# Four weight matrices, each by one transfer onto 96 partitions, in a decode kernel (attention and MLP mixer, one core)

## The chip, the cores and the metric

The kernel runs on one core of one Trainium2 chip. The metric is the device time of one execution in microseconds (us). Before the change it is 215.7 us, the median of three runs (215.67 to 217.24).

## The reference

Four tokens (batch B = 4, one position, D = 576) go through a layer norm. The result `xn` feeds two branches, whose outputs are added to `x`.

```python
xn  = layernorm(x)
out = x + A(xn) + Bm(xn)
# A: sliding-window attention over a cache, 32 query heads, 16 KV heads, Dh = 128
q = xn @ wq                      # 576 x 4096
k, v = last 2048 positions of k_cache, v_cache   # of 8192
A = softmax(q k^T / sqrt(128)) v @ wo            # 4096 x 576
# Bm: mixer MLP
h  = gelu(layernorm(xn) @ w1)    # 576 x 576
hs = shift(h) @ w2               # one position only: every shifted part is zero
x1 = xn + hs
Bm = x1 + gelu(layernorm(x1) @ w3) @ w4          # 576 x 4608, 4608 x 576
```

With one position the shifted `h` is all zeros, so the product with `w2` has a zero operand; the kernel still loads `w1` and `w2` and multiplies. All data is bf16.

## The kernel before, in words

The kernel is written as a list of operations for each engine (`prog`), each with a sort key, a list of events to wait for and an event that it signals. `add` (L163) and `add_dma` (L167) fill the lists, the lists are sorted by key (L543), and each engine then runs its list in order. An operation that waits holds everything behind it on its engine. Keys, not the order in the file, set the order of the work. All transfers but that of `x` and half of the output are issued by SP, in one queue.

**Buffers.** `kring` (L69) and `vring` (L70) are rings with four slots each (NKS, NVS); a slot has UE = 8192 bf16 for each of 128 partitions and holds one KV head of K or V, 2 MB. `regB` (L72) holds transposed K (`ktbuf`, 16 slots). Before the heads arrive the same memory holds the weights: `wq`, `w1` and `w2` lie in the V ring (L79 to L90), `w3` in `regB` (L77, L78), later `wo` in the K ring (L81) and `w4` in the V ring (L242).

**A weight with 576 rows on 128 partitions.** 576 is four and a half times 128. Rows 0 to 511 go to 128 partitions, four consecutive rows each (the "main" part); the last 64 rows are split into halves of columns, so that (row, half) makes 128 short rows (the "rag" part, `rag_src`, L178). `wq` and `w3` come by three transfers each (rows r = 0 and 1, rows 2 and 3, the rag; L215 to L218 and L221 to L224), `w1` and `w2` by two (L219, L220). The stationary operand has to match: `ragsrc` (L103) holds the last 64 columns of the normed tokens twice, spread over even and odd columns, with zeros between. Two copies in `ln_ops` (L266, L267) write it behind each of the three norms, and `pe_xT` (L270) makes six small transposes, four of the main part and two of `ragsrc`.

**Order of the first part.** On SP: `wq`, `w1`, `w2`, `w3` (keys -20 to -8), K0 to K3 without a wait, then K4 and on, each waiting until its slot was transposed (L230 to L232). V0 goes in after K8 (V0_AFTER), V1 to V15 after K15; V0 to V2 wait for `hs1`, as the weights lie in those slots, and V4 and on wait for the head that used the slot before (L236). `wo` follows V3. On TensorE: transposes of the first and second norm's result, `q` in five pieces that each wait for their part of `wq` (`pe_q`, L286, L299), the transposes of q, `hT` (`w1`, L472) and `hs0`, `hs1` (`w2`, L481), the transposes of the third norm, `h2` in five pieces (`pe_h2`, L501), then `pe_zeroS` (L318), which opens the score sums in PSUM and waits for all that used those banks. Then the loop over K: for each head 64 transposes (`pe_T`, L327), which VectorE and ScalarE copy to `ktbuf` (`evac`, L337), and 16 score matmuls (`pe_SC`, L343) for the head before.

**After K.** One softmax for all heads (L374 to L410), then the loop over V (`pe_PV`, L412), `wo` (`pe_AO`, L443) and `w4` (L527), and the two halves of the output.

## Time and profile before

| | |
|---|---|
| median of three runs | 215.7 us |
| the profiled execution | 215.64 us |
| its span, first to last instruction | 214.4 us |
| instructions | 5735 |
| TensorE matmul busy | 143.2 us, 67% |
| weight load busy | 109.1 us, 51% |
| VectorE, ScalarE, GpSimd busy | 84.5, 59.1, 10.0 us |
| read from HBM | 88.49 MB |
| mean clock granted to TensorE | 0.785 |

How to read it. Times are microseconds unless marked ns. PE is TensorE's matmul, PEld its weight load, DVE VectorE, ACT ScalarE, POOL GpSimd, SP SyncE; SPq is the instructions by which SP issues transfers. L332 is line 332 of the kernel. "out<-in" are the tensors written and read, xN the number of instructions. A time and a duration at the start of a line are the start from the beginning of the span and the length; in brackets stands how long the engine sat idle before and what ended that. The chain of work that ended last is followed back from the last instruction, at each step to what released it. The DMA and GB/s rows give the span in 40 equal slices of 5.36 us. A stretch of the windows view gives, in order, the bounds, the length, busy time and count of each engine (PE, PEld, DVE, ACT, POOL), the granted clock, the share of the 16 DMA engines that was busy, and GB/s.

### The profile page before, as it was taken

Reading aid. Unit: us, or ns where it says so; the run is one execution under the profiler, and the core shown is the slowest. Engines: PE = TensorE matmul, PEld = TensorE weight load, DVE = VectorE, ACT = ScalarE, POOL = GpSimd, SP = SyncE. Lnnn points to the kernel's source line nnn. Section 1 sums busy time; section 2 is a strip of 40 time slices with the busy share of each in tenths; the row PEclk is TensorE's granted clock in tenths of the full one; section 3 lists DMA queues with packets and bytes.
Section 4 is the critical chain, followed back from the end, with each engine's and each line's share of the span. In section 5 each row is a group of like instructions: output and inputs, shape, how many; then the busy total and the mean of one; then the engine's idle time right before and its main releaser. Section 6 shows DMA issues by size and latency. Waiting matters only on the chain.

```text
span 214.4 us, 5735 instructions
## 1 busy us (share of the span) xinstructions
PE 143.2 (67%) x2646; PEld 109.1 (51%) x2648; DVE 84.5 (39%) x162; ACT 59.1 (28%) x71; POOL 10.0 (5%) x34
## 2 busy tenths in 40 slices
PE   0368375999999993999999719813343443973655
PEld 0115223777788883788877604813343443463523
DVE  5502603666666663466666479411111112100000
ACT  2000302566555553365666653000000000000000
POOL 8101000000010000000000000000000000000000
PEclk9999755999999999699999985555555555585589
DMA  6999999999999999999999999999999999999992
GB/s 245 434 395 439 440 410 437 428 408 431 428 431 422 431 428 434 422 434 423 431 425 431 428 407 411 424 427 431 419 434 431 431 419 434 428 434 421 424 412 113
DMA packets 7697, 88.63 MB, mean 413 GB/s; under 512 B 764, under 2 KB 1032, under 8 KB 2824
## 3 DMA queue, kind: packets, MB, share of 16 engines
q1 hardware_dynamic: 7672, 88.50, 97.8%
q8 instruction: 7, 0.11, 0.2%
q14 instruction: 2, 0.02, 0.0%
q10 hardware_dynamic: 16, 0.01, 0.0%
HBM read 88.49 MB, written 0.00 MB: 413 GB/s over the span
## 4 chain that ended last, share of the span: by engine, by line
DMA 53%; PE 36%; DVE 4%; SPq 4%; issue 2%; ACT 0%
DMA vring<-in_A_v_cache_dram 25%; PE ps L332 23%; DMA kring<-in_A_k_cache_dram 21%; PE ps L348 7%; DMA vring<-in_B_w_dram 7%; PE ps L416 5%; SPq L174 4%; DVE PTb L382 1%; DVE rmax L374 1%; DVE regB L340 1%; PE ps L441 1%; DVE PTs L390 1%; PE ps L405 0%; ACT P_sb L379 0%; DVE out_sb L539 0%
## 5 line engine op out<-in xcount | busy, mean ns | idle before, releaser
L340 DVE COPY regB<-ps 128x1024 bf16<-128x1024 bf16 x80 | 52.3, 687 | 34.7 <-PE ps L332 32.9
L332 PEld LDWEIGHTS ps<-perm_k,kring 128*128 128x128 bf16 x1024 | 58.7, 99 | 12.6 <-issue 8.7
L332 PE MATMUL ps<-perm_k,kring 128*128 128x128 bf16 x1024 | 62.1, 222 | 4.2 <-DMA kring<-in_A_k_cache_dram 4.2
L339 ACT ACTIVATE regB<-ps 128x1024 bf16<-128x1024 bf16 x48 | 47.7, 1023 | 41.4 <-PE ps L332 41.4
L416 PE MATMUL ps<-PTg,vring 128*128 128x8 bf16 x1024 | 29.2, 168 | 33.3 <-DMA vring<-in_A_v_cache_dram 31.4
L416 PEld LDWEIGHTS ps<-PTg,vring 128*128 128x128 bf16 x1024 | 28.1, 103 | 34.5 <-DMA vring<-in_A_v_cache_dram 24.3
L424 DVE TENSOR_TENSOR OTn<-ps,rinvB 128x8 bf16<-128x8 f32 x16 | 2.7, 167 | 57.3 <-PE ps L416 57.2
L540 ACT ACTIVATE out_sb<-ps 4x288 bf16<-4x288 f32 x1 | 0.4, 402 | 81.2 <-PE ps L441 81.2
L348 PE MATMUL ps<-regB,Qs 128*32 128x512 bf16 x272 | 18.7, 395 | 4.6 <-issue 3.5
L348 PEld LDWEIGHTS ps<-regB,Qs 128*32 128x32 bf16 x272 | 6.6, 97 | 10.8 <-issue 6.2
L393 DVE TENSOR_TENSOR PTg<-PTs,bmask 128x512 bf16<-128x512 bf16 x16 | 10.7, 682 | 0.0
L370 POOL COPY Qs<-Qpad 128x128 bf16<-128x128 bf16 x16 | 4.6, 296 | 93.5 <-PE ps L348 81.4
L441 PE MATMUL ps<-kring,ORT 128*4 128x288 bf16 x64 | 7.7, 431 | 0.7 <-DVE ORT L458 0.7
L441 PE MATMUL ps<-vring,h2T_sb 128*4 128x288 bf16 x72 | 5.3, 299 | 2.8 <-DMA vring<-in_B_w_dram 2.8
L511 PE MATMUL ps<-regB,x1nT 128*32 128x432 bf16 (+1 forms) x60 | 5.4, 522 | 2.1 <-DMA regB<-in_B_w_dram 1.6
L274 PE MATMUL ps<-ident_bf,xn_bf 4*128 4x4 bf16 x8 | 0.5, 169 | 8.8 <-DVE ragsrc L267 8.8
L296 PE MATMUL ps<-vring,xnT 128*32 128x512 bf16 x40 | 4.6, 629 | 1.8 <-DMA vring<-in_A_wq_dram 1.8
L441 PEld LDWEIGHTS ps<-kring,ORT 128*4 128x4 bf16 x64 | 3.8, 121 | 3.9 <-DVE ORT L458 0.9
L441 PEld LDWEIGHTS ps<-vring,h2T_sb 128*4 128x4 bf16 x72 | 3.0, 87 | 5.3 <-DMA vring<-in_B_w_dram 4.0
L383 PE MATMUL ps<-PTb,perm_p 128*128 128x512 bf16 x3 | 1.8, 608 | 4.9 <-DVE PTb L382 4.8
L274 PEld LDWEIGHTS ps<-ident_bf,xn_bf 4*128 4x128 bf16 x8 | 0.4, 112 | 8.8 <-POOL ones_f L210 6.3
L524 DVE STREAM_TRANSPOSE h2T_sb<-PTb 128x1152 bf16<-128x1152 bf16 x1 | 1.4, 1378 | 8.4 <-ACT PTb L521 8.4
(88 smaller groups left out, 61.7 us busy)
## 6 DMA issues: line engine op xcount, KB each, us to landing
kring<-in_A_k_cache_dram SPq DMA_DIRECT2D x16, 2048.0 KB, 16.1
vring<-in_A_v_cache_dram SPq DMA_DIRECT2D x16, 2048.0 KB, 17.6
regB<-in_B_w_dram SPq DMA_DIRECT2D x2, 2304.0 KB, 21.3
kring<-in_A_wo_dram SPq DMA_DIRECT2D x1, 4608.0 KB, 24.1
vring<-in_A_wq_dram SPq DMA_DIRECT2D x2, 2048.0 KB, 9.5
vring<-in_B_w_dram SPq DMA_DIRECT2D x2, 2016.0 KB, 15.7
vring<-in_B_w_dram SPq DMA_DIRECT2D x2, 576.0 KB, 13.8
vring<-in_B_w_dram SPq DMA_DIRECT2D x1, 864.0 KB, 14.7
```

Of the source, the lines that this page charges most:

```text
L174: e.dma_start(o_, i_).then_inc(S[skey], 16)
L296: ins = e.matmul(Qps[32 * j:32 * j + 32, k, :], lhsT=x_, rhs=w, start=(r == 0), stop=(r == 4), tile_position=(0, 32 * j))
L332: ins = e.transpose(tb[n % NTB][:, t, :], kring[:, g % NKS, 8 * k + t, :], perm_k[:])
L339: return "act", lambda e: e.activation(out=ktbuf[:, n % NKT], in_=src, func=ACTF.Copy)
L340: return "dve", lambda e: e.tensor_copy(out=ktbuf[:, n % NKT], in_=src)
L348: ins = e.matmul(Sps[32 * b:32 * b + 32, c4, :].rearrange("p (t i) -> p t i", t=16), lhsT=Qs[:, g % 4, b, :], rhs=kttile[:, t0:t0 + 16, b, :],
L370: P(lambda e, g=g: e.tensor_copy(out=Qs[:, g % 4], in_=Qpad[:, g]), waits=(["qT"] if g == 0 else []) + ([f"SC{g - 4}"] if g >= 3 else []), ...
L393: add("dve", lambda e, g=g: e.tensor_tensor(out=PTg[:, g % NPG], in0=PTs[:, :, 2 * g:2 * g + 2].unsqueeze(2).to_broadcast([128, NT, B, 2]) ...
L416: ins = e.matmul(OTps(g), lhsT=vring[:, g % NVS, t, :], rhs=PTg[:, g % NPG, t].rearrange("p b e -> p (b e)"), start=(t == 0), stop=(t == N ...
L424: add("dve", lambda e, g=g: e.tensor_tensor(out=OTn[:, 8 * g:8 * g + 8], in0=OTps(g), in1=rinvB[:, 8 * g:8 * g + 8], op=ALU.mult), waits=[ ...
L441: return e.matmul(ACC[h], lhsT=lhsT, rhs=rhs, start=start, stop=stop, tile_position=(0, 32 * h))
L511: ins = e.matmul(H2ps[k][32 * j:32 * j + 32, :], lhsT=x_, rhs=w, start=(r == 0), stop=(r == 4), tile_position=(0, 32 * j))
```

## The change

`wq`, `w1`, `w2` and `w3` each come by one transfer: 576 = 96 x 6, so 96 partitions (`KP`) get six consecutive rows each, and partitions 96 to 127 nothing. There is no rag part, and `ragsrc`, its memset and its copies go. Every product with these weights is a sum over six rows instead of four and a remainder. `wq` lies in slots 1 to 3 of the K ring, `w1` and `w2` in slot 0, `w3` in the V ring. So K0 waits for `hs1`, K1 to K3 wait for `q`, and V0 to V3 for `h2`. `q` and `h2` are one operation each, which waits for the whole weight. Slots 8 to 15 of `ktbuf`, which held `w3` before, are set to zero by GpSimd (`kt_zero`), and `pe_zeroS` waits for that: the first score matmuls read them.

```diff
-        regB_t = sb("regB", [128, max(NKT * 1024, W3E)], BF16)
+        regB_t = sb("regB", [128, NKT * 1024], BF16)
...
+        w3_sb = vring_t[0:KP, 0:6 * F].rearrange("p (r n) -> p r n", r=6)
+        wq_sb = kring_t[0:KP, UE:UE + 6 * Hq * Dh].rearrange("p (r n) -> p r n", r=6)
+        w1_sb = kring_t[0:KP, 0:6 * D].rearrange("p (r n) -> p r n", r=6)
+        w2_sb = kring_t[0:KP, 6 * D:12 * D].rearrange("p (r n) -> p r n", r=6)
...
-        xnT = sb("xnT", [128, 6, 32], BF16)
+        xnT = sb("xnT", [KP, 6, 32], BF16)
...
-        def rag_src(w_ap):
-            return w_ap[512:576, :].rearrange("r (h n) -> (r h) n", h=2)
+        def rows6(w_ap):
+            return w_ap.rearrange("(p r) n -> p r n", r=6)
...
-        P(lambda e: e.memset(ragsrc[:], 0.0), sig="rag_zero", key=-97)
...
+        P(lambda e: e.memset(ktbuf[:, 8:16, :], 0.0), sig="kt_zero", key=-88)
...
-        for r in (0, 2):
-            ev_wq += 2 * [add_dma([(wqmain[:, r:r + 2, :], wq_src[:, r:r + 2, :])], ("wq", r), (), -20 + r)]
-        ev_wq.append(add_dma([(wqrag, rag_src(A_wq))], ("wq", 4), (), -15))
...
+        ev_wq, ev_w1, ev_w2, ev_w3 = [add_dma([(d_, rows6(s_))], nm, (), -20 + k) for k, (nm, d_, s_) in enumerate(
+            (("wq", wq_sb, A_wq), ("w1", w1_sb, B_w1), ("w2", w2_sb, B_w2), ("w3", w3_sb, B_w3)))]
...
-                                [f"T{8 * (g - NKS) + 7}"] if g >= NKS else [], g))
+                                [f"T{8 * (g - NKS) + 7}"] if g >= NKS else ["hs1" if g == 0 else "q"], g))
...
-            w = [f"PV{g - NVS}"] if g >= NVS else (["hs1"] if g < WQ_SLOTS else [])
+            w = [f"PV{g - NVS}"] if g >= NVS else ["h2"]
...
-            add("dve", lambda e: (e.tensor_copy(out=ragsrc[:, idx, 0, 0:128:2], in_=dst[:, 512:D]),
-                                  e.tensor_copy(out=ragsrc[:, idx, 1, 1:128:2], in_=dst[:, 512:D]))[1],
-                waits=[f"{tag}_n", "rag_zero"], sig=tag, key=k0 + 0.05)
...
+        def pe_q(e):
+            ins = None
+            for k in range(2):
+                for r in range(6):
+                    for j in range(4):
+                        c0 = 1024 * j + 512 * k
+                        ins = e.matmul(Qps[32 * j:32 * j + 32, k, :], lhsT=xnT[:, r, :], rhs=wq_sb[:, r, c0:c0 + 512],
+                                       start=(r == 0), stop=(r == 5), tile_position=(0, 32 * j))
+            return ins
+        add("pe", pe_q, waits=[ev_wq, "xnT"], sig="q", key=-30)
...
-        add("pe", pe_zeroS, waits=["zeros_bf", "perm_k", "gelu2", "gelu_h", "qT", "x1nT", "x1"], sig="zeroS", key=-1)
+        add("pe", pe_zeroS, waits=["zeros_bf", "perm_k", "gelu2", "gelu_h", "qT", "x1nT", "x1", "kt_zero"], sig="zeroS", key=-1)
...
+        add("pe", pe_h2, waits=[ev_w3, "x1nT", "qT"], sig="h2", key=KW)
```

`pe_hT`, `pe_hs` and `pe_h2` change in the same way as `pe_q`: one loop over r = 0 to 5.

## The prediction

> **What bounds the kernel now.** I read the page first: the span, the DMA rate in 40 slices, the queue table.

> ```profile
> span 214.4 us, 5735 instructions
> GB/s 245 434 395 439 440 410 437 428 408 431 428 431 422 431 428 434 422 434 423 431 425 431 428 407 411 424 427 431 419 434 431 431 419 434 428 434 421 424 412 113
> q1 hardware_dynamic: 7672, 88.50, 97.8%
> ```

> Every slice but the first and the last moves 395 to 440 GB/s, and nearly all of the traffic is in one queue, SP's. 88.5 MB have to pass through it. The end therefore moves with two things only: a hole in that queue, or a change of the pace at which it drains. The chain of work that ended last shows who feeds whom:

> ```profile
> 8.87 27.18 DMA kring<-in_A_k_cache_dram
> 36.05 0.13 issue
> 36.18 1.83 PE ps L332 x16
> 38.02 0.98 PE ps L348 x16
> 38.99 3.71 PE ps L332 x64
> ...
> 43.99 3.71 PE ps L332 x64
> ```

> K0 was issued at 8.87 and landed at 36.05: 27 us, nearly all of it behind the weights. From then on TensorE takes one K head every 5.00 us (38.99 to 43.99). The pace in that stretch of the span (last column GB/s, before it the share of the 16 DMA engines):

> ```profile
> 36.00:66.00 30.00, 28.58 (x470) 23.95 (x471) 18.43 (x29) 16.41 (x17) 1.78 (x6) 0.97 1.01 427
> ```

> A head of K is 2048 KB (row below), 2.097 MB, so 4.91 us at 427 GB/s: DMA and TensorE run almost level, TensorE 0.09 us a head slower, and V0, put in after K8, gives TensorE the time back. SP's own list of issues (start, length of the run, how many) tells how far ahead the queue is filled:

> ```profile
> 0.81 1.34 SPq L174 DMA_DIRECT2D vring<-in_A_wq_dram  x3
> ...
> 8.87 53.45 SPq L174 DMA_DIRECT2D kring<-in_A_k_cache_dram  x9
> 62.36 0.60 SPq L174 DMA_DIRECT2D vring<-in_A_v_cache_dram  x1
> ...
> 116.69 0.39 SPq L174 DMA_DIRECT2D kring<-in_A_wo_dram  x1
> 134.27 48.11 SPq L174 DMA_DIRECT2D vring<-in_A_v_cache_dram  x12
> ```

> K0 to K3 were issued together, V0 after K8, wo once K14 was transposed, V4 once V0 was used up. The first slice's 245 GB/s are 1.31 MB, 3.0 us at 434, so the first byte moved at about 2.3, 1.5 us after the first issue.

> **The change part by part.** *The four weights on 96 rows.* Their sizes, with those of K and wo (KB each, then the time from issue to landing):

> ```profile
> kring<-in_A_k_cache_dram SPq DMA_DIRECT2D x16, 2048.0 KB, 16.1
> regB<-in_B_w_dram SPq DMA_DIRECT2D x2, 2304.0 KB, 21.3
> kring<-in_A_wo_dram SPq DMA_DIRECT2D x1, 4608.0 KB, 24.1
> vring<-in_A_wq_dram SPq DMA_DIRECT2D x2, 2048.0 KB, 9.5
> vring<-in_B_w_dram SPq DMA_DIRECT2D x2, 576.0 KB, 13.8
> regB<-in_B_w_dram SPq DMA_DIRECT2D x1, 576.0 KB, 25.8
> vring<-in_A_wq_dram SPq DMA_DIRECT2D x1, 512.0 KB, 12.5
> vring<-in_B_w_dram SPq DMA_DIRECT2D x2, 72.0 KB, 13.5
> ```

> The weights (wq 4096 + 512, w1 and w2 1152 + 144, w3 4608 + 576) are 11088 KB, 11.35 MB; at 427 GB/s 26.6 us. All of these transfers lie on 128 partitions, as K and V do. The new ones put the same bytes on 96, a third more on each. The trace has no large transfer on fewer than 128 partitions, so I bound the cost. If the 16 engines set the pace and share the 96 rows (six each), the stream still takes 26.6 us: cost 0. If it is the partition that sets the pace, nothing in this trace shows one filled faster than 427 / 128 = 3.34 GB/s; 96 of them take 320 GB/s, the stream 35.5 us: cost +8.9. If, beyond that, two engines keep meeting at the same partitions' input and halve each other, it is up to twice, 53.2 us: cost +26.6. I take +8.9, because the one rate that the trace shows, on every large transfer, belongs to 128 evenly filled partitions, and a gap there is not refilled: the queue is full all the way to the end.

> [...]

> *Fewer transfers.* Ten issues become four, and the 72 KB ones with short rows go. That SP issues sooner is worth nothing, since its first transfer still starts at 0.81 and the queue is never empty. The short rows cost pace: slices three and six (395 and 410 GB/s beside 434 to 440) lose 0.52 and 0.33 us of their 5.36. Not all of it is theirs; between 0 and 0.85 I take 0.4 gained.

> *The matmul work.* Six rows instead of four and a remainder: wq 40 matmuls to 48, w1 and w2 10 to 12 each, w3 60 to 72, and each starts only when its whole weight is in, no longer in pieces:

> ```profile
> 9.36 1.90 PE L296 MATMUL ps<-vring,xnT 128*32 128x512 bf16 x16
> 13.04 2.75 PE L296 MATMUL ps<-vring,xnT 128*32 128x512 bf16 x24 [1.78 <-DMA vring<-in_A_wq_dram]
> 17.62 1.12 PE L476 MATMUL ps<-vring,xn2T 128*4 128x288 bf16 x4
> 19.97 1.05 PE L484 MATMUL ps<-vring,hs_inT 128*4 128x288 bf16 x4
> 21.47 0.29 PE L485 MATMUL ps<-vring,hs_inT 128*4 128x288 bf16 x1
> 28.63 2.11 PE L511 MATMUL ps<-regB,x1nT 128*32 128x432 bf16 x24 [1.12 <-DMA regB<-in_B_w_dram]
> 31.19 1.15 PE L511 MATMUL ps<-regB,x1nT 128*32 128x432 bf16 x12 [0.45 <-DMA regB<-in_B_w_dram]
> 32.39 1.26 ACT L521 ACTIVATE PTb<-ps 128x432 bf16<-128x432 f32 x3 [5.07 <-PE ps L511]
> 34.10 1.49 PE L321 MATMUL ps<-zeros_bf 128*128 128x512 bf16 x3 [1.76 <-ACT PTb L521]
> ```

> The last piece of w3 is used from 31.19; it comes at 31.2 - 0.4 + 8.9 = 39.7. Then 72 matmuls at 2.11 / 24 = 0.088 us, 6.3 us, to 46.0; the gelu (1.26, with its hand-over 1.4) to 47.4; the zeroing of the scores, which ended 1.9 us after the gelu (33.65 to 35.59), to 49.3. K0 has been there since 39.7 + 4.9 = 44.6. So the first transpose of K is at 49.3 instead of 36.18, 13.1 us late, of which only 8.5 are the stream's. What hides the other 4.6: K4 is issued when K0 is transposed, 5.6 us after the first transpose (36.18 to 38.99 plus three quarters of 3.71), at 54.9, while K3 lands at 39.7 + 4 x 4.9 = 59.3. The queue has 4.4 us in hand, less the 1.5 from issue to first byte, and loses 0.09 a head until V0. After that TensorE has this slack as well:

> ```profile
> PE ps L332 <- DMA kring<-in_A_k_cache_dram: 4.2, 2, 3.6
> ```

> At V0 it stood still for 3.6 us; that wait shrinks to nothing and the K phase ends some 13.1 - 3.6 = 9.5 late. V4, issued at 134.27, goes out at 143.8; wo, issued at 116.69 and 24.1 us under way, lands near 140.8 + 8.5 = 149.3. So V4 is in time and the end moves with DMA alone. Without this cover each late microsecond would be one at the end.

> *The waits.* K0 now waits for hs1, K1 to K3 for q, V0 for h2. Behind K0 on SP stand K1 to K3 and everything later, and TensorE's first transpose waits for K0. hs1 ended at 21.76 (21.47 + 0.29). wq's last piece, issued at about 1.7 and 12.5 under way, was in at 14.2; with the stream at 4/3 wq is in at 14.2 + 3.7 = 17.9. Sixteen matmuls took 1.90, so 48 take at most 5.7, and q ends at 23.6 instead of 15.8 (13.04 + 2.75). The four matmuls more of w1 and w2 before hs1 add 2 x 0.235 (17.62 to 19.97 is ten) and 2 x 0.18 (19.97 to 21.76): 0.8. hs1 comes at 21.76 + 7.8 + 0.8 = 30.4, long before w3 leaves the queue at about 39. Cost nothing; w3 behind it in the queue is the cover. V0, issued at 62.36, and h2, done at 46.0, do not meet.

> *GpSimd and VectorE.* One memset and six copies go, a memset of 128 x 8192 comes.

> ```profile
> 2.19 2.31 DVE L404 COPY bmask<-bmask 128x4 f32<-128x4 f32 x1
> 2.65 1.82 POOL L193 MEMSET Qpad<- 128x2080 bf16 x1
> 8.28 0.42 DVE L264 TENSOR_SCALAR xn_bf<-xn_bf,mv,rstd 4x576 bf16<-4x576 bf16 x1
> ```

> At 1.82 us for 2080 columns the new one takes 7.2, from about 5.4 to 12.6. The tiny copy that lasted 2.31 us and ended with the Qpad memset suggests that VectorE's SBUF copies stand still meanwhile; then the second norm's last step slips from 8.28 to 12.6, and the transposes before q to about 13.4. wq lands at 14.2 at the earliest: cost nothing, with 0.8 us in hand, or 4.5 with the slow stream. Each norm is also 0.3 to 0.5 us shorter without its copies, which the wait for wq or w3 hides.

> Sum, against the profiled execution's own 215.64 us (span 214.4 and 1.2 around it; the median of the runs shown is 215.7): 215.6 + 8.9 - 0.4 = **224.1 us**.

> **The rivals.**

> *No loss: the engines share 96 rows as well as 128.* For it: the DMA share is 1.01 in the quoted stretch, so all 16 engines are busy, and six rows each is an even split. Against it: no row shows them at this pace into fewer partitions. It decides if wq lands before about 15 us. q then ends at 14.2 + 5.7 = 19.9, hs1 is at 21.76 + 4.1 + 0.8 = 26.7, K0's first byte at about 28.2 and w3 through at 31.2 - 0.4 = 30.8, so the queue has no hole; the transposes start 13.1 - 8.5 = 4.6 us late and are covered as above. Time 215.6 - 0.4 = 215.2: not slower.

> *The new gate becomes the bound.* The same fast stream, but q late, because the memset holds up both norms instead of one: the first norm then ends after 12.6, the second needs its 2 us once more, q starts at about 16 and hs1 is at 28.5. From about 29 on K0 comes after w3 has left, and each microsecond is a hole. Against it: the first norm's end precedes the memset in the list of before. Time 215.2 + 0 to 4, about 217.

> *Uneven meeting.* Rows are 48 and 54 KB long, so an engine stays on one row for longer than now (16 and 18 KB); engines that meet stay together, the last of 16 sets the landing, and the fast ones run ahead into K and then starve. [...] Against: any arbitration that spreads. Up to twice: 215.2 + 26.6 = 242; halfway from the forecast, 233.

> **How the numbers follow.** Forecast (even slowing, 220 to 229) 0.46; no loss 0.17; the gate 0.06; uneven meeting 0.27; anything else, such as more than twofold slowing, 0.04. No loss and half of the gate lie within 1% (what a measurement of this kernel can tell from no change): 0.17. Over 1% faster would need more than the 0.85 us of short rows: 0.02. Slower: 0.81. The range goes from the no-loss case with the whole 0.85 us, 214.8, to 240, which leaves out the top of the uneven case; the forecast's own is 220 to 229.

> **What would show it.** Right: fewer GB/s, some 320, in the slices up to about 38 us and 427 to 434 after; q starting near 18, the last w3 matmuls from about 39.7, the first K transpose near 49; TensorE's wait at V0 gone. Wrong: wq in at 14 (no loss), K0's issue after w3 has landed (gate), or w3 in after 45 (uneven). If holes appear in K's slices after 50, the cover that I counted on was too thin.

## The result and the profile after

The changed kernel takes 242.96 us, the median of five runs (241.75 to 244.83), beside 215.72 us before (215.67 to 217.24). The ratio is 1.1235, with a 95% interval of 1.1164 to 1.1306: slower by 12%. The profiled execution took 241.91 us with a span of 240.6. The forecast was 224.1 us, the range 214.8 to 240.0; the result lies outside it. In the ratios here and below, executions more than 1.5% above the fastest of the same kernel are left out.

The page of the changed kernel, span, DMA share and rate in 40 slices (now of 6.0 us each):

```profile
span 240.6 us, 5773 instructions
DMA  9796979879999999999999999999999999999992
GB/s 238 155 261 135 354 156 269 175 150 376 428 417 425 429 425 433 425 422 430 433 426 433 425 425 428 408 413 437 419 430 430 428 425 433 422 433 428 427 411 115
```

From the tenth slice on this is the picture of before. The first nine slices, in which the weights come, swing between 135 and 354 (a long packet seems to be counted whole where it starts: between 25 and 30 us the windows view gives a DMA share of 1.57) and are on average far below it. The windows view evens this out when a stretch takes in the whole weight stage. Here it is of the kernel before, up to the last weight, and then of the changed kernel; the last columns are the share of the 16 DMA engines and GB/s:

```profile
2.00:31.00 29.00, 14.88 (x134) 6.62 (x134) 10.56 (x34) 3.87 (x8) 4.82 (x14) 0.88 0.99 414
```

```profile
2.00:56.40 54.40, 13.42 (x98) 7.47 (x98) 16.32 (x28) 3.88 (x8) 10.97 (x14) 0.84 0.97 213
60.00:90.00 30.00, 27.64 (x431) 21.44 (x424) 16.59 (x25) 14.74 (x17) 1.48 (x5) 0.89 1.01 426
90.00:120.00 30.00, 28.04 (x472) 23.11 (x470) 18.99 (x30) 17.41 (x18) 1.76 (x6) 1.00 1.01 428
```

The reader is to see two columns together. In the weight stage the engines are busy for 0.97 of the time, as good as always, yet they move 213 GB/s instead of 414. They are not idle or starved: together they work at half their pace. With K the same engines move 426 to 428. The issues, KB each and time to landing:

```profile
vring<-in_B_w_dram SPq DMA_DIRECT2D x1, 5184.0 KB, 53.5
kring<-in_A_wq_dram SPq DMA_DIRECT2D x1, 4608.0 KB, 25.2
kring<-in_B_w_dram SPq DMA_DIRECT2D x2, 648.0 KB, 28.4
```

wq takes 25.2 us from issue to landing; in the kernel before, its last piece was in at about 14.2. The timelines of TensorE and of SP's issues carry it on:

```profile
26.05 5.31 PE L267 MATMUL ps<-kring,xnT 96*32 96x512 bf16 x48 [9.51 <-DMA kring<-in_A_wq_dram]
56.41 5.95 PE L477 MATMUL ps<-vring,x1nT 96*32 96x432 bf16 x72 [15.45 <-DMA vring<-in_B_w_dram]
63.73 1.89 PE L291 MATMUL ps<-zeros_bf 128*128 128x512 bf16 x4 [1.36 <-ACT PTb L486]
65.41 1.57 PE L302 MATMUL ps<-perm_k,kring 128*128 128x128 bf16 x16
37.55 53.72 SPq L162 DMA_DIRECT2D kring<-in_A_k_cache_dram  x9
158.97 49.64 SPq L162 DMA_DIRECT2D vring<-in_A_v_cache_dram  x12
```

w3 is in at 56.41 instead of 31.19, 25.2 us late. The first transpose of K is at 65.41 instead of 36.18, 29.2 late; by V4's issue (158.97 instead of 134.27) the lateness is 24.7, and most of the difference went into TensorE's waits for K, which shrank from 4.2 us (3.6 of them at V0) to 0.9; the end is 26.3 late (241.91 - 215.64). Of these 26.3 us, 25.2 are there when w3 lands. What the V phase adds, 1.6 us, is less than the spread of the five runs (3.1 us), and I do not explain it.

### The profile page after: what moved, and what is told of

The parts are those of the page before. It is cut to its first block, busy times and chain, and to the rows that moved or that the text cites. A ratio compares the mean times of both kernels' runs of the same rounds, so it can differ in the third digit from the quotient of the medians.

```text
span 240.6 us, 5773 instructions
## 1 busy us (share of the span) xinstructions
PE 146.8 (61%) x2672; PEld 111.8 (46%) x2672; DVE 90.2 (38%) x156; ACT 59.4 (25%) x71; POOL 16.1 (7%) x34
## 3 DMA queue, kind: packets, MB, share of 16 engines
q1 hardware_dynamic: 6680, 88.49, 97.8%
## 4 chain that ended last, share of the span: by engine, by line
DMA 46%; PE 39%; another core or an unknown queue 6%; DVE 5%; issue 2%; ACT 1%
DMA vring<-in_A_v_cache_dram 23%; PE ps L302 20%; DMA kring<-in_A_wq_dram 10%; DMA kring<-in_A_k_cache_dram 7%; DMA vring<-in_B_w_dram 6%; PE ps L318 6%; PE ps L386 4%; PE ps L477 2%; PE ps L267 2%; PE ps L446 1%; DVE PTb L352 1%; DVE rmax L344 1%; PE ps L291 1%; PE ps L454 1%
## 5 line engine op out<-in xcount | busy, mean ns | idle before, releaser
L302 PEld LDWEIGHTS ps<-perm_k,kring 128*128 128x128 bf16 x1024 | 58.0, 98 | 9.0 <-issue 7.3
L386 PEld LDWEIGHTS ps<-PTg,vring 128*128 128x128 bf16 x1024 | 28.3, 103 | 36.4 <-DMA vring<-in_A_v_cache_dram 24.8
L318 PE MATMUL ps<-regB,Qs 128*32 128x512 bf16 x272 | 17.8, 381 | 4.2 <-issue 2.9
L477 PE MATMUL ps<-vring,x1nT 96*32 96x432 bf16 (+1 forms) x72 | 6.0, 526 | 15.4 <-DMA vring<-in_B_w_dram 15.4
L477 PEld LDWEIGHTS ps<-vring,x1nT 96*32 96x32 bf16 x72 | 2.6, 146 | 18.3 <-DMA vring<-in_B_w_dram 15.5
L267 PE MATMUL ps<-kring,xnT 96*32 96x512 bf16 x48 | 5.3, 630 | 9.5 <-DMA kring<-in_A_wq_dram 9.5
L252 PE MATMUL ps<-ident_bf,xn_bf 4*96 4x4 bf16 x12 | 1.9, 268 | 14.7 <-DVE xn_bf L244 14.7
L489 DVE STREAM_TRANSPOSE h2T_sb<-PTb 128x1152 bf16<-128x1152 bf16 x1 | 1.4, 1378 | 22.5 <-ACT PTb L486 22.5
L252 PEld LDWEIGHTS ps<-ident_bf,xn_bf 4*96 4x96 bf16 x12 | 1.7, 221 | 14.7 <-POOL regB L198 12.6
L411 PE MATMUL ps<-vring,h2T_sb 128*4 128x288 bf16 x72 | 6.4, 343 | 1.6 <-DMA vring<-in_B_w_dram 1.6
L267 PEld LDWEIGHTS ps<-kring,xnT 96*32 96x32 bf16 x48 | 1.7, 141 | 12.3 <-DMA kring<-in_A_wq_dram 9.6
L198 POOL MEMSET regB<- 128x8192 bf16 x1 | 6.9, 6921 | 0.0
## 6 DMA issues: line engine op xcount, KB each, us to landing
kring<-in_A_k_cache_dram SPq DMA_DIRECT2D x16, 2048.0 KB, 15.1
vring<-in_A_v_cache_dram SPq DMA_DIRECT2D x16, 2048.0 KB, 17.6
vring<-in_B_w_dram SPq DMA_DIRECT2D x1, 5184.0 KB, 53.5
kring<-in_A_wq_dram SPq DMA_DIRECT2D x1, 4608.0 KB, 25.2
kring<-in_A_wo_dram SPq DMA_DIRECT2D x1, 4608.0 KB, 25.6
vring<-in_B_w_dram SPq DMA_DIRECT2D x2, 2016.0 KB, 16.1
vring<-in_B_w_dram SPq DMA_DIRECT2D x1, 864.0 KB, 14.7
```

The costliest lines, as they stand in the source:

```text
L198: P(lambda e: e.memset(ktbuf[:, 8:16, :], 0.0), sig="kt_zero", key=-88)
L252: ins = e.transpose(XTps[idx][:, r, :], v[:, r, :], ident_bf[0:B, 0:B])
L267: ins = e.matmul(Qps[32 * j:32 * j + 32, k, :], lhsT=xnT[:, r, :], rhs=wq_sb[:, r, c0:c0 + 512], start=(r == 0), stop=(r == 5), tile_posit ...
L302: ins = e.transpose(tb[n % NTB][:, t, :], kring[:, g % NKS, 8 * k + t, :], perm_k[:])
L318: ins = e.matmul(Sps[32 * b:32 * b + 32, c4, :].rearrange("p (t i) -> p t i", t=16), lhsT=Qs[:, g % 4, b, :], rhs=kttile[:, t0:t0 + 16, b, :],
L386: ins = e.matmul(OTps(g), lhsT=vring[:, g % NVS, t, :], rhs=PTg[:, g % NPG, t].rearrange("p b e -> p (b e)"), start=(t == 0), stop=(t == N ...
```

## The experiments

Two theories were set against each other after the result. Theory P: it is the partitions; with 96 of them the engines meet at the same inputs of the on-chip memory. (An input here is a path by which data of the DMA engines enters a group of partitions; that there are such shared paths is part of the theory, and the last run tests it.) The rivals: L, it is the long packets (48 and 54 KB instead of 16 and 18); S, it is where the engines read in HBM; and later E, an engine is simply slow in any load that does not have 128 partitions.

**Two rows per transfer** (`e1_two_rows`). The diffs of this part show the changed pieces of lines.

```diff
-add_dma([(d_, rows6(s_))], nm, (), -20 + k)
+add_dma([(d_[:, r:r + 2, :], rows6(s_)[:, r:r + 2, :]) for r in (0, 2, 4)], nm, (), -20 + k)
```

> The changed kernel with each of the four weights in three transfers of two rows per partition, still on 96 partitions. A packet is then 16 or 18 KB, as in the kernel before, instead of 48 or 54 KB. Theory P (the partitions: with 96 of them the 16 engines meet two by two at the same input): nothing changes, w3 in at about 56 us and 243 us in all. Rival L (the long rows: a packet of 48 KB moves at half the rate of one of 16 KB): the stream is back at 427 GB/s, w3 in at about 31 us, 216 to 219 us in all. Rival S (the source: many engines reading HBM at a distance of 48 KB from each other): as P.

Measured: 237.2 us (one run), w3 used from 52.6. The windows view of this run:

```profile
2.00:50.00 48.00, 13.64 (x98) 7.57 (x98) 16.32 (x28) 3.88 (x8) 10.97 (x14) 0.87 1.01 235
```

With packets of 16 and 18 KB the stream runs at 235 GB/s, a tenth faster than the 213 with 48 and 54 KB, and far from 427. Long packets have a share: w3 is used 3.8 us earlier, and the end comes 4.7 us earlier (237.2 beside 241.91), of the 26 us in all. L is not the main cause. P said "nothing changes" and missed that share.

**The same bytes flat on 128 partitions** (`e2_flat128`). Each weight still comes by one transfer, behind the same gates, with the same memset and the same instructions. `flat128` holds the parts of the same buffers that the weights then fill, over all 128 partitions; the products with `w1`, `w2` and `w3` change as the one with `wq`.

```diff
-add_dma([(d_, rows6(s_))], nm, (), -20 + k)
+add_dma([(flat128[k], s_.rearrange("r n -> (r n)").rearrange("(p m) -> p m", p=128))], nm, (), -20 + k)
...
-rhs=wq_sb[:, r, c0:c0 + 512]
+rhs=wq_sb[:, r % 4, c0:c0 + 512]
```

> The changed kernel, each weight still by one transfer of the same bytes, but spread flat over 128 partitions (36 KB of wq, 5 KB of w1 and w2, 40.5 KB of w3 on each). The products take four of the rows that then lie on a partition twice or once, so q, the MLP and the output are not the reference's; all instructions are those of the changed kernel. Theory P: the stream is back at 427 GB/s, wq in near 14 us, w3 near 31, 216 to 218 us in all (the upper end if the long memset holds the first norm and K0 waits for hs1). Rival L: 36 and 40 KB are still long, so the stream stays near half rate and the time near 243. Rival S: somewhere between, the distance of the engines in HBM is another.

Measured: of ten executions six took 216.1 to 217.3 us and four 219.5 to 221.1. The ratio to the kernel before (215.66 to 215.90 in 13 executions beside them) is 1.0033 (1.0018 to 1.0047). Windows and issues of this run:

```profile
2.00:30.00 28.00, 11.62 (x98) 6.74 (x98) 16.32 (x28) 1.95 (x6) 10.97 (x14) 0.97 0.97 409
vring<-in_B_w_dram SPq DMA_DIRECT2D x1, 5184.0 KB, 28.7
kring<-in_A_wq_dram SPq DMA_DIRECT2D x1, 4608.0 KB, 13.6
```

wq lands after 13.6 us instead of 25.2, w3 after 28.7 instead of 53.5, with packets of 36 and 40 KB. This settles the main point: of the 12% all but 0.3% hang on 96 against 128 partitions. The gates, the single wait for a whole weight, the added matmuls, the memset and the fewer transfers cost, all together, 0.3%.

**The memset moved behind the norms** (`e3_flat128_late_memset`): as e2, with `waits=["xn2T"]` on the long memset.

> As the run before (the same rows left out of the products), with the long memset of the transposed-K buffer moved behind the transposes of the second norm, so that no norm waits for it. If the memset opened a hole by way of the norms, q and hs1, this is 0.5 to 2 us faster than the run before and at 215 to 216; if the gate on K0 is covered as in the prediction's first rival, the two are the same.

Timelines, first of e2, then of this run:

```profile
5.60 6.84 DVE L246 TENSOR_SCALAR xn_bf<-x_sb,mv,rstd 4x576 bf16<-4x576 bf16 x1
16.48 5.21 PE L269 MATMUL ps<-kring,xnT 96*32 96x512 bf16 x48
26.25 37.44 SPq L164 DMA_DIRECT2D kring<-in_A_k_cache_dram  x9
```

```profile
5.60 0.42 DVE L246 TENSOR_SCALAR xn_bf<-x_sb,mv,rstd 4x576 bf16<-4x576 bf16 x1
14.62 5.13 PE L269 MATMUL ps<-kring,xnT 96*32 96x512 bf16 x48 [4.50 <-DMA kring<-in_A_wq_dram]
24.32 39.99 SPq L164 DMA_DIRECT2D kring<-in_A_k_cache_dram  x9
```

The last step of the first norm takes 0.42 us, or 6.84 while the memset runs. Without that q waits for wq alone, starts 1.9 us earlier, and K0 is issued 1.9 us earlier. The profiled executions took 215.45 us against 216.67. But the timed runs do not bear out a gain: four executions here took 215.45 to 219.43, ratio 1.0115 (1.0058 to 1.0171) from three of them with a wide spread, against 1.0033 for e2. The expected 0.5 to 2 us are seen in one pair of profiles only; whether the memset costs time stays open, and so does the spread of 4 to 5 us in both variants, beside 0.24 in the kernel before.

**The loads by themselves** (`e4_probe`). Only loads, one at a time, each awaited.

```diff
+sp.dma_start(buf[0:96, 0:24576], src(kf, 96, 24576)).then_inc(sem, 16)
+sp.wait_ge(sem, 32)
```

> No attention and no MLP: only large loads into one buffer, one at a time, each awaited, and an output of zeros. 48 KB per partition from the K cache to 128 partitions, to 96 (0 to 95), 96 (32 to 127), 112, 80, 64 (0 to 63), 64 (64 to 127), 32, 16 and 120; then 16 KB per partition to 96 and to 128; then wq's bytes as 36 KB to 128 and 48 KB to 96. Theory P: 128 partitions at about 427 GB/s whatever the row (14.7 us of stream for 48 KB, and about 2 us around it), 96 at about 210 (22.5 us) whatever the row length, the source and the first partition; 64 and 32 no better than 210. Rival L: 128 partitions of 48 KB at half rate too (29.5 us), 96 of 16 KB at full rate (3.7 us). Rival S: the rate goes with the source, so the two loads of wq differ from those of the K cache with the same partitions.

SP's waits in this run. The wait at one line is for the load issued at the line before: L27 waited for 128 partitions, L29 for 96, L31 for 96 (32 to 127), L33 for 112, L35 for 80, L37 and L39 for 64, L41 for 32, L43 for 16, L45 for 120; L47 and L49 for 16 KB on 96 and on 128; L51 and L54 for wq's bytes on 128 and on 96.

```profile
SPq L45 <- DMA buf<-in_A_k_cache_dram: 31.9, 1, 31.9
SPq L29 <- DMA buf<-in_A_k_cache_dram: 24.1, 1, 24.1
SPq L54 <- DMA buf<-in_A_wq_dram: 24.0, 1, 24.0
SPq L33 <- DMA buf<-in_A_k_cache_dram: 23.9, 1, 23.9
SPq L31 <- DMA buf<-in_A_k_cache_dram: 23.9, 1, 23.9
SPq L35 <- DMA buf<-in_A_k_cache_dram: 20.2, 1, 20.2
SPq L37 <- DMA buf<-in_A_k_cache_dram: 17.6, 1, 17.6
SPq L39 <- DMA buf<-in_A_k_cache_dram: 17.2, 1, 17.2
SPq L27 <- DMA buf<-in_A_k_cache_dram: 17.2, 1, 17.2
SPq L51 <- DMA buf<-in_A_wq_dram: 13.1, 1, 13.1
SPq L41 <- DMA buf<-in_A_k_cache_dram: 9.6, 1, 9.6
SPq L43 <- DMA buf<-in_A_k_cache_dram: 9.2, 1, 9.2
SPq L47 <- DMA buf<-in_A_k_cache_dram: 8.8, 1, 8.8
SPq L49 <- DMA buf<-in_A_k_cache_dram: 7.4, 1, 7.4
```

128 partitions of 48 KB (6.29 MB) need 17.2 us; 96 of them, a quarter fewer bytes, need 24.1. 64 partitions need as long as 128. If about 1.8 us of each wait is not stream (an estimate: 26.7 GB/s, a sixteenth of the 427 of K's stream, move one packet of 48 KB in 1.8 us, and a load of one packet, in the last run below, took 3.6), the rates are:

| partitions (48 KB each) | 16 | 32 | 64 | 80 | 96 | 112 | 120 | 128 |
|---|---|---|---|---|---|---|---|---|
| GB/s, worked out | 106 | 202 | 199 | 214 | 212 | 249 | 196 | 409 |

Of the loads of 32 to 120 partitions none is faster than 249 GB/s, and there is no even slope up to 128: there is a step between 120 and 128. L falls once more (48 KB on 128 is fast, 409 GB/s), and S falls: wq's bytes behave as the K cache's (13.1 us on 128, 24.0 on 96).

**Only w3 on 96, only w3 on 128** (`e5_only_w3_96`, `e6_only_w3_128`): e2 with a choice by name, `(flat128[nm], flat source) if nm in FLAT else (d_, rows6(s_))`.

> The changed kernel with wq, w1 and w2 flat on 128 partitions (the products with them take four of the rows that lie there, so the output is not the reference's) and only w3 on 96. Theory P (96 partitions take data at about 205 GB/s, and the end moves by exactly what the stream loses): w3's 5.31 MB take 25.9 us instead of 12.4, 13.5 more, so about 229.5 us in all, w3 in at about 45. Rival (one of the gates or the single waits holds the end as well): more than that; rival (the loss is a matter of one of the two rings, or of wq alone): 216 or 242.

> The opposite: wq, w1 and w2 on 96 partitions, only w3 flat on 128 (its products take four rows, the output is not the reference's). Theory P: 6.04 MB at 205 GB/s instead of 427 take 29.5 us instead of 14.1, 15.3 more, but w1 and w2 with their 7 KB rows lost less in the changed kernel (landings 2.6 us apart, 260 GB/s), so about 14, 230 us in all. In sum with the run before: the 26 us of the whole change, to within 2 us. Rivals as there.

Measured: 228.5 and 230.5 us (one run each). The starts of the products with w3, first e5, then e6:

```profile
44.17 5.50 PE L481 MATMUL ps<-vring,x1nT 96*32 96x432 bf16 x72 [11.59 <-DMA vring<-in_B_w_dram]
```

```profile
44.60 5.17 PE L481 MATMUL ps<-vring,x1nT 96*32 96x432 bf16 x72 [2.23 <-DMA vring<-in_B_w_dram]
```

Against the profiled e2 (216.67) they cost 11.9 and 13.8 us, 25.7 in sum; the whole change costs 241.91 - 216.67 = 25.2. These two runs and the last one were made on another chip than e1 to e4; the one execution of the kernel before on that chip took 216.92 us, and measured from it the two cost 11.6 and 13.6. V4's issue, which comes before the spread of the V phase, says the same: 145.32 and 147.81 beside 134.17 in e2, 11.15 and 13.64 late, 24.8 in sum, as much as the whole change (158.97). So the loss adds up, nearly by bytes (w3 is 5.31 MB, the others 6.04), no gate adds to it, and it is a matter of both rings alike. Most of it passes to the end: in e5 w3 is used 13.2 us later than in e2 (30.95), and the end is 11.9 later.

**One, two, four, eight partitions** (`e7_probe_ports`).

```diff
+sp.dma_start(buf[0:8, :], src(8)).then_inc(sem, 16)
...
+sp.dma_start(buf[0:32:4, :], src(8)).then_inc(sem, 16)
```

> No attention and no MLP, an output of zeros: loads of 48 KB per partition, one at a time. To partition 0 alone, 4 alone, 64 alone; 0 and 1; 0 and 64; 0 and 32; 0 to 3; 0 to 7; every fourth of 0 to 31 (8 partitions); every fourth of 0 to 63 (16 partitions); then 0 to 63 and 64 to 127 as two transfers behind each other in SP's queue; the same two at the same time in SP's and ScalarE's queues; then all 128 in one. Theory P (several partitions share one input that takes about 27 GB/s; neighbours share it, and so do partitions 32 apart): one partition alone, and 0 and 64, and every fourth of 0 to 31 run at about 27 GB/s per engine (1.8 us a packet); 0 and 1, 0 and 32, and every fourth of 0 to 63 at half (3.6 us); 0 to 3 at a quarter (7.2 us); 0 to 7 at a quarter as well. Two halves behind each other about 31 us, at the same time clearly less (16 to 24), all 128 in 16 us. Rival E (an engine works at half rate in any load that does not have 128 partitions): every load but the last at about 3.7 us a packet, and the two halves 31 us in either order. [...]

SP's waits again, 48 KB per partition. L28 waited for partition 0, L30 for 4, L32 for 64; L34 for 0 and 1, L36 for 0 and 64, L38 for 0 and 32; L40 for 0 to 3, L42 for 0 to 7, L44 for every fourth of 0 to 31, L46 for every fourth of 0 to 63; L49 for the two halves in one queue, L55 for the two halves in two queues, L59 for all 128.

```profile
SPq L49 <- DMA buf<-in_A_k_cache_dram: 31.9, 1, 31.9
SPq L55 <- DMA buf<-in_A_k_cache_dram: 31.8, 1, 31.8
SPq L59 <- DMA buf<-in_A_k_cache_dram: 17.2, 1, 17.2
SPq L42 <- DMA buf<-in_A_k_cache_dram: 8.5, 1, 8.5
SPq L40 <- DMA buf<-in_A_k_cache_dram: 8.2, 1, 8.2
SPq L46 <- DMA buf<-in_A_k_cache_dram: 5.7, 1, 5.7
SPq L38 <- DMA buf<-in_A_k_cache_dram: 5.6, 1, 5.6
SPq L34 <- DMA buf<-in_A_k_cache_dram: 5.5, 1, 5.5
SPq L44 <- DMA buf<-in_A_k_cache_dram: 3.9, 1, 3.9
SPq L36 <- DMA buf<-in_A_k_cache_dram: 3.9, 1, 3.9
SPq L30 <- DMA buf<-in_A_k_cache_dram: 3.7, 1, 3.7
SPq L32 <- DMA buf<-in_A_k_cache_dram: 3.6, 1, 3.6
SPq L28 <- DMA buf<-in_A_k_cache_dram: 3.6, 1, 3.6
```

One expectation of P failed: the two halves from two queues at the same time take 31.8 us, as long as behind each other (31.9). Why is not shown: the trace does not name the engine of a packet.

## Why the prediction was wrong

**The step that failed** is the first, "The four weights on 96 rows": I took the middle of three values, +8.9 us, where +25.2 was measured at w3's landing. The stream did not slow in the proportion 128 to 96, to 320 GB/s, but to 213, half. I had divided the rate by the partitions as if the loss went with how many are left out. The table above shows that it does not: 80 partitions or 96, 212 to 214 GB/s; even 120 are slow. The value that fits is the third, +26.6, for which I had supposed that two engines keep meeting at one input and halve each other; I had named it and not taken it. In the small loads of the last run it matters which partitions a load goes to, not only how many: eight take 8.5 us side by side and 3.9 on every fourth. The 213 GB/s on 96 partitions are 8 x 26.7 = 214, as if the 16 engines halved each other two by two. That is an estimate, and that they meet at inputs is inferred: which rows each engine is given is not shown by any run, and the runs with 96 partitions take them all in a row (0 to 95 or 32 to 127), so that none tells the sharing from the mere number. What is shown is that 96 against 128 partitions is the cause.

**The rival that came nearest** had the size, not the form. "Uneven meeting" gave up to 242, and 241.91 came in the profiled execution. But it said that the last of 16 engines sets the landing, which no run shows, and that the fast ones run ahead and starve. In the row 2 to 56.4 of the windows the 16 engines are busy at 0.97 while 213 GB/s move: none runs ahead and starves, they are slow together. So the agreement of its number comes from the bound, twice the time, and not from its story. I gave this rival 0.27 and cut my range below its upper end, at 240.

**No loss** was excluded by wq's landing, at 26.0 instead of before 15. Its premise held, all 16 engines were busy, 0.97 of the time; what it had wrong is that a busy engine keeps its pace (213 GB/s here, 427 at a share of 1.01 with K in the kernel before).

**Fewer transfers** gained little if anything: in e2, which has them on 128 partitions, w3 is used from 30.95 instead of 31.19, 0.2 us earlier where I took 0.4, and the kernel as a whole is 0.3% slower. No run has them alone.

**The matmul work** was right. From w3's landing to the first transpose I had 9.6 us; it was 65.41 - 56.41 = 9.0. The cover held too: the waits for K, 3.6 us of them at V0, shrank as predicted,

```profile
PE ps L302 <- DMA kring<-in_A_k_cache_dram: 0.9, 1, 0.9
```

from 4.2 us to 0.9, and after the weights the rate is 426 and 428 GB/s, with no hole.

**The waits** were right. K0 was issued at 37.55, right after hs1, and w3 was in the queue until 56, so the gate cost nothing; in e2, where w3 is fast, K0 goes out at 26.25 and w3 is used from 30.95, and the kernel is within 0.3%.

**The memset** held up the first norm, not the second. In the list of before its place comes 0.4 us behind the first norm's last step (which ends at 5.72). But the memset of `ragsrc` ahead of it, 0.73 us, goes, and with the start at 5.4 that I had worked out myself it comes ahead of that end. In the trace of the changed kernel it starts just before the norm's last step:

```profile
5.36 6.92 POOL L198 MEMSET regB<- 128x8192 bf16 x1
5.60 6.84 DVE L244 TENSOR_SCALAR xn_bf<-x_sb,mv,rstd 4x576 bf16<-4x576 bf16 x1
```

The cover that I named, wq's landing, hid it here (q could have started at 16.6 and wq came at 26.05). In e2 it shows: q starts at 16.48, 1.9 us behind wq.

## What to carry to other kernels

In a kernel that is bound by its loads, let each large load go to all 128 partitions: on the chips of these runs, loads of 32 to 120 partitions ran at 190 to 250 GB/s, loads of 128 at about 410 alone and 427 in a stream. That all 16 engines are busy does not tell their pace (0.97 at 213 GB/s, 0.99 at 414); read the share of the engines and the GB/s together. Here a matrix of 576 rows was better cut into 128 x 4.5, with a clumsy remainder (215.72 us), than into 96 x 6 (242.96). And when the bounds of a cost lie at 0, +9 and +27 with no row between them, the range has to reach the far one.

## What the runs showed that I had not expected

The step at 128 partitions: 120 partitions need 31.9 us for 5.9 MB, 128 need 17.2 for 6.3. On 96 partitions the packet's length mattered: 235 GB/s with 16 and 18 KB, 213 with 48 and 54. Two queues did not help: 31.8 us for two halves at once, 31.9 in a row. And a VectorE step of 0.42 us became one of 6.84 behind a GpSimd memset.
